# A gated recurrence with a slot mixture behind it: fillers placed elsewhere, two weight loads issued two units earlier, and the last weight loaded in two halves

## The chip, the cores and the metric

The kernel runs on one core of a Trainium2 chip. The metric is the device time of one execution in microseconds. The time before is the median of five runs.

## The reference

The inputs are `x` and `f_logit` of 4 x 5056 x 256 (batch, time, channel), a lower bound per channel, and the parameters of a mixture of experts with 32 slots: `phi` (256 x 32), eight first weights (256 x 1024) and eight second weights (1024 x 256). All are 32-bit floats.

```python
sig = 1.0 / (1.0 + np.exp(-f_logit))
f = lower_bound + (1.0 - lower_bound) * sig
for t in range(S):
    h = f[:, t] * h + (1.0 - f[:, t]) * x[:, t]
    y[:, t] = h
x = y.reshape(B * S, D)
logits = x @ phi
d = softmax over all tokens of logits          # per slot
slot_input = d.T @ x                           # 32 x 256
for e in range(8):                             # four slots each
    slot_out[e] = np.maximum(slot_input[e] @ w1[e], 0.0) @ w2[e]
c = softmax over the slots of logits           # per token
out = c @ slot_out
```

The softmax over tokens, and so the experts, need all tokens first. The kernel therefore has three stages: the recurrence with the slot sums, a short middle part with the experts, and the output, which writes 20224 rows of 256 values.

## The kernel before

**Units.** Time is cut into ten groups of 512 steps, and each group into four units, one for each batch element: 40 units (`n_unit`), numbered n. One pass of the main loop handles one n, with work of neighbouring units overlapped by hand; the order of instructions on every engine is the order in which the code issues them (`tc.manual_schedule()`).

In pass n the code calls, among others: `load(n + 6)` for two units at a time, which issues the reads of f_logit and x on SP's queue (lines 182 to 190, tiles `f_t` and `x_t`, three buffers each); `gate`, a sigmoid on ScalarE (line 200, tile `s_t`); `enter(n + 3)`, the product of gate and x on GpSimd, called POOL in the profile (line 211, tile `u_t`); `s_to_channels` and `u_to_channels`, transposes on TensorE (lines 213 to 226); `decay` on ScalarE (line 249); `scan`, the recurrence itself on VectorE (line 259, tile `h`); `to_tokens` and `keep_tokens`, transposes back and their copy (lines 272 and 289, tiles `hp` and `ht`).

**Exponential blocks.** The logits of two groups at a time go through one exponential (`exps`, line 312, tile `etall`). Then `weights_to_tokens` transposes them on TensorE (line 324), VectorE copies them (line 327), and `slots` adds the products with the tokens into `slot_ps` (line 353). In the loop this happens once in eight units: the transposes in a pass with n % 8 = 2, the slot sums of the block's two groups in the two passes behind it.

**Fillers.** `idle(k)` (lines 163 to 166) issues k matmuls that nobody reads. They write the second half of the bank whose first half is `slot_ps`. `spin(dst, k, w)` (lines 135 to 138) does the like with w columns, on the weight that is loaded first. The loop's fillers stand behind the transposes of a unit, at lines 473 to 476.

**Weights.** `load_w(i)` issues the read of one expert weight on POOL's queue, with a cast from 32 to 16 bits, 1 MB read and 512 KB written. Weights 0 to 7 are the first weights of the experts, 8 to 15 the second ones. `W_AT` says how many are issued in which pass, behind `enter` in POOL's order.

**The middle part.** Behind the loop, the last slot sums are scaled (line 541), the first weights are applied (line 559), and then the second ones: experts 0 to 3 together (line 595), and experts 4 to 7 one after the other (line 605, j = 0 to 3, eight matmuls each over the eight parts fc of the weight). Between j = 1 and j = 2 stand the last row sums (line 336) and `SPINS` fillers. Then VectorE scales the result (line 619, `slot_out`), and POOL makes the two-row form of it (line 621, `slot_bd`).

**The output.** `pieces`, `couple`, `rest` and `whole` multiply the exponentials with `slot_out` or `slot_bd` on TensorE (lines 639, 688 and 710), scale the rows on VectorE (lines 629 and 693) and ScalarE (lines 633 and 699), and issue the writes on SP's queue (lines 665, 676, 702 and 719). The PSUM bank in which the fillers write is given back to these tiles.

Of the kernel before, what the change touches and what calls it, by code (L numbers as in the profile page):

```python
# [18 lines left out]
def kernel(  # L19
# [10 lines left out]
    nc = tc.nc  # L30
    B, S, D = x.shape
    E = moe_w1.shape[0]
    F = moe_w1.shape[2]
    NS = moe_phi.shape[1]
    SPE = NS // E
    P = 128
    DC = D // P
    FC = F // P
# [3 lines left out]
    n_unit = n_grp * B  # L42
# [27 lines left out]
    ident = consts.tile([P, P], BF16, name="ident")  # L70
# [13 lines left out]
    def rep_constants(b):  # L84
        blk = ident_f[ds(b * NS, NS), ds(b * NS, NS)]
        nc.gpsimd.tensor_copy(rep[ds(b * NS, NS)], blk.unsqueeze(1).broadcast_to([NS, B, NS]))
# [33 lines left out]
    w2_r = moe_w2.rearrange("e (p fc) d -> e p fc d", p=P)  # L120
# [5 lines left out]
    w2_sb = [wts.tile([P, FC, D], BF16, name=f"w2_sb{e}") for e in range(E)]  # L126

    def load_w(i):
        if i < E:
            nc.gpsimd.dma_start(out=w1_sb[i], in_=w1_r[i])  # L130
        else:
            nc.gpsimd.dma_start(out=w2_sb[i - E], in_=w2_r[i - E])  # L132


    def spin(dst, k, w):
        for _ in range(k):
            nc.tensor.matmul(dst[:, ds(0, w)], w1_sb[0][:, 0, :P], w1_sb[0][:, 0, :w],
                             start=True, stop=True, skip_group_check=True)

    SPINS = 28  # L140
    W_AT = {17: 1, 25: 1, 30: 1, 31: 1, 32: 1, 33: 2, 34: 1, 36: 8}
    w_next = [0]
    ctx.enter_context(tc.manual_schedule())

# [3 lines left out]
    with tc.tile_pool(name="sp2", bufs=3) as sp2, \  # L148
# [9 lines left out]
        slot_bank = pslot.tile([P, 2, D], F32, name="slot_ps")  # L158
        slot_ps = slot_bank[:, 0]

        rep_bf = rep.rearrange("p b s -> p (b s)").bitcast(BF16)

        def idle(k, first=False):
            for i in range(k):
                nc.tensor.matmul(slot_bank[:, 1], ident, rep_bf,  # L165
                                 start=first and i == 0, stop=False, skip_group_check=True)
        xs, fs, sts, uts, pss, psus, hs, hps, hts, lgs, ets = ({} for _ in range(11))

        def tokens(src, n, k):
# [58 lines left out]
        def s_to_channels(n):  # L228
            if n % 2 == 0:
                pss[n // 2] = psp.tile([P, 2, P, R], F32, name="sp", tag="sp")  # L230
            to_channels(n, pss[n // 2][:, n % 2], sts[n // 2][:, n % 2],
                        sts[n // 2][:, 0, R3])
# [31 lines left out]
        SINGLE = 6  # L264
# [28 lines left out]
        def batch_of(g):  # L293
            return [g & ~1, g | 1] if g < n_grp - 2 else [g]
# [64 lines left out]
        def unit(f, m):  # L359
            if 0 <= m < n_unit:  # L360
                f(m)

        def group(f, m):
            if 0 <= m < n_unit and m % B == B - 1:
                f(m // B)

        def batch(f, m, i):
            m -= i
            if 0 <= m < n_unit and m % B == B - 1:
                gs = batch_of(m // B)  # L370
                if m // B == gs[-1] and i < len(gs):
                    f(gs[i])
# [52 lines left out]
        for n in range(n_unit):  # L425
            if n < SINGLE - 2:
                if n:
                    unit(to_tokens, n - 1)
                    unit(u_to_channels, n + 1)
                s_to_channels(n + 2)  # L430
                if n + 3 < SINGLE:
                    gate(n + 3, 1)
                decay(n + 2, 1)
                if n + 3 == SINGLE:
                    gate(n + 3)
                if n % 2 == 0:
                    unit(load, n + AHEAD)
                unit(enter, n + 3)
                rep_constants(n)
            else:  # L440
                end = n >= n_unit - 6
                if n % 2 == 0:
                    unit(load, n + AHEAD)
                    if n == SINGLE - 2:
                        to_tokens(n - 1)
                        keep_tokens(n - 1)
                    if not end:
                        unit(gate, n + 4)
                else:
                    unit(decay, n + 1)  # L450
                    if n == n_unit - 5:
                        gate(n + 3)
                        exps(odd - 1)
                if not end and n != n_unit - 7:
                    group(exps, n - 2)

                unit(enter, n + 3)
                for _ in range(W_AT.get(n, 0)):
                    load_w(w_next[0])
                    w_next[0] += 1  # L460

                if n == n_unit - 2:
                    unit(u_to_channels, n + 1)
                if n != SINGLE - 2:
                    unit(to_tokens, n - 1)
                if n == n_unit - 2:
                    keep_tokens(n - 1)
                if n % 2 == 0:
                    unit(s_to_channels, n + 2)
                    unit(s_to_channels, n + 3)  # L470
                if n != n_unit - 2:
                    unit(u_to_channels, n + 1)
                if n in (n_unit - 5, n_unit - 4):
                    idle(4)
                elif SINGLE - 2 < n < n_unit - 4 and n % (2 * B) in (1, 2, 5, 6, 7):
                    idle(5, n == SINGLE - 1)
                if n == n_unit - 2:
                    tail = psp.tile([P, 2, G], F32, name="tail", tag="sp")
                    rs_ps = tail[:, 0, ds(0, n_grp * R * B)].rearrange(
                        "p (q b) -> p q b", b=B)  # L480
                    late_ps, odd_ps = (
                        tail[:, 1].bitcast(BF16)[:, ds(i * R * P, R * P)].rearrange(
                            "p (r s) -> p r s", r=R) for i in range(2))
                    logits(odd)
                    exps(odd)
                    slots(odd - 1)
                    spin(tail[:, 1], 1, G)
                    odd_weights()
                elif not end:
                    group(logits, n - 1)  # L490
            if n == n_unit - 1:
                logits(last, [0, 1, 2])
                late_exps([0, 1, 2])
                row_sums(0)
                late_weights([0, 1, 2], nc.scalar.copy)

            unit(scan, n)
            if n not in (SINGLE - 2, n_unit - 2):
                unit(keep_tokens, n - 1)
            if n == n_unit - 3:  # L500
                weights_to_tokens(odd - 1)
                slots(odd - 2)
            elif not n >= n_unit - 6:
                group(weights_to_tokens, n - 3)
                batch(slots, n - 4, 0)
                batch(slots, n - 4, 1)
        hid, wide = (ld.tile([P, 2, R, D], F32, name=i, tag="x_t") for i in ("hid", "wide"))
        hid = hid.rearrange("p u r d -> p (u r d)").bitcast(BF16)[:, ds(0, FC * E // 2 * NS)]
        wide = wide.rearrange("p u r d -> p (u r d)").bitcast(BF16)[:, ds(0, FC * E // 2 * P)]
# [19 lines left out]
        for o in range(DC):  # L529
            nc.tensor.matmul(sin_ps[:, o], slot_v[:, o], rep[:, 0],  # L530
                             start=True, stop=True, skip_group_check=True)

    with tc.tile_pool(name="ew", bufs=1) as ew, \
# [18 lines left out]
        for q in range(E // Q):  # L552
            hi = ew.tile([P, F], BF16, name=f"hi{q}")
            for k in range(2):
                hi_ps = (psu.tile([P, H], F32, name="hi_ps", tag="up") if q == 0 else
                         pbig.tile([P, H], F32, name="hi_ps", tag=f"hi_ps{k}"))
                for o in range(DC):
                    for j in range(Q):
                        nc.tensor.matmul(hi_ps[ds(j * NS, NS)], sin[:, o],
                                         w1_sb[q * Q + j][:, o, ds(k * H, H)],  # L560
                                         start=(o == 0), stop=(o == DC - 1),
                                         skip_group_check=True)
# [30 lines left out]
        for e in range(Q):  # L593
            for fc in range(FC):
                nc.tensor.matmul(so4_ps[ds(fc % 4 * NS, NS), :], hid[:, fc, e],
                                 w2_sb[e][:, fc],
                                 start=(e == 0 and fc < 4),
                                 stop=(e == Q - 1 and fc >= FC - 4),
                                 skip_group_check=True)
# [3 lines left out]
        for j in range(Q):  # L603
            for fc in range(FC):
                nc.tensor.matmul(so_ps, wide[:, fc, j].rearrange("p b s -> p (b s)"),
                                 w2_sb[Q + j][:, fc],
                                 start=j == 0 and fc == 0, stop=j == Q - 1 and fc == FC - 1,
                                 skip_group_check=True)
            if j == 0:
                nc.tensor.matmul(so_ps, rep2, so4, start=False, stop=False,  # L610
                                 skip_group_check=True)
            if j == 1:
                for i in range(1, len(blocks)):
                    row_sums(i)
                q = n_grp * R - 1
                spin(tail[:, 1], SPINS, NS)
                nc.vector.reciprocal(rrow[:, wide_r:q], rs_ps[:, wide_r:q])
                nc.vector.reciprocal(rrow[:, q, ds(0, B // 2)], rs_ps[:, q, ds(0, B // 2)])
        nc.vector.tensor_scalar_mul(slot_out, so_ps, rcs)  # L619
        for u in range(2):  # L620
            nc.gpsimd.tensor_scalar_mul(slot_bd[:, u], slot_out, parity[:, ds(u, 1)])  # L621
# [139 lines left out]
```

## Time and profile before

| | us |
|---|---|
| median of five runs | 202.58 |
| lowest and highest | 201.61 and 203.11 |
| the profiled execution, its own time | 201.61 |
| its span | 199.8 |

| engine | busy us | share of the span |
|---|---|---|
| TensorE, matmuls (PE) | 141.7 | 71% |
| TensorE, weight loads (PEld) | 102.8 | 51% |
| VectorE (DVE) | 142.7 | 71% |
| ScalarE (ACT) | 137.9 | 69% |
| GpSimd (POOL) | 101.9 | 51% |

A profile gives for each engine its busy time, in 40 slices of the span a digit for the busy share in tenths, and for each group of instructions the mean duration and what ended the wait before it. The row PEclk is the clock that TensorE was granted, in tenths of full speed. The DMA row is the mean share of 16 DMA rings that were busy. A DMA with a cast counts in GB/s with the bytes that it writes. The chain that ended last follows the execution back from its end, from each step to what released it. Busy shares are means over three unlike stages, so the stages are read one by one.

### The profile page before, as it was taken

What the parts mean: (1) busy time and instruction counts of PE and PEld (TensorE: products, weight loads), DVE (VectorE), ACT (ScalarE), POOL (GpSimd) and SP (SyncE); (2) the same over time, 40 slices, a digit from 0 to 9 for tenths busy, and PEclk for the clock granted to TensorE, in tenths of its full rate; (3) what the DMA queues carried; (4) which work ended last, traced back from release to release, by engine and by line L of the source; (5) the groups of instructions that cost most, each with busy time, mean ns of one, the idle gap of its engine ahead of it and who ended that gap; (6) DMA issues with size and microseconds to landing.
All of it is one profiled execution on the core that took longest, in us unless ns stands there. A gap on an engine that the chain in (4) does not pass through costs nothing.

```text
span 199.8 us, 3263 instructions
## 1 busy us (share of the span) xinstructions
PE 141.7 (71%) x1201; PEld 102.8 (51%) x1201; DVE 142.7 (71%) x164; ACT 137.9 (69%) x194; POOL 101.9 (51%) x76
## 2 busy tenths in 40 slices
PE   0587564986988959777888778999679999970000
PEld 0365443965776847665776666667653533420000
DVE  1669878699999998999999999342167887850000
ACT  2688675899998997999996694621057889990000
POOL 2589595874999296983998779900030000000000
PEclk9999999699999988999999999999985555555555
DMA  5999999999999999999999999999529999999994
GB/s 177 417 420 420 420 421 415 420 420 417 416 419 419 335 394 421 419 405 307 419 415 275 252 217 197 216 212 215 111 98 394 416 449 430 420 423 436 453 420 213
DMA packets 17615, 70.76 MB, mean 354 GB/s; under 512 B 2096, under 2 KB 3120, under 8 KB 16704
## 3 DMA queue, kind: packets, MB, share of 16 engines
q1 hardware_dynamic: 15120, 62.13, 76.1%
q0 software_dynamic: 2336, 8.42, 21.1%
q8 instruction: 9, 0.15, 0.3%
q14 instruction: 6, 0.05, 0.1%
q10 hardware_dynamic: 144, 0.00, 0.0%
HBM read 58.23 MB, written 20.71 MB: 395 GB/s over the span
## 4 chain that ended last, share of the span: by engine, by line
PE 28%; DVE 22%; DMA 18%; issue 11%; POOL 6%; ACT 4%; SPq 0%; DVEq 0%; ACTq 0%; POOLq 0%
DVE h L259 18%; PE op L688 12%; DMA w_sb<-in_moe_w_dram 10%; DMA f_t<-in_f_logit_dram 8%; POOL u_t L211 4%; PE hp L272 3%; PE sp L226 3%; PE op L639 3%; DVE ht L289 3%; PE up L226 2%; POOL w_sb L132 2%; ACT oc L699 1%; PE slot_ps L165 1%; ACT a L249 1%; DVE et L327 1%
## 5 line engine op out<-in xcount | busy, mean ns | idle before, releaser
L211 POOL TENSOR_TENSOR u_t<-s_t,x_t 128x1024 bf16<-128x1024 bf16 (+1 forms) x39 | 82.2, 2124 | 24.8 <-ACT s_t L200 19.6
L259 DVE TENSOR_TENSOR_SCAN h<-a,h,up 128x512 bf16<-128x512 f32 (+1 forms) x72 | 86.0, 1249 | 4.0 <-PE up L226 2.4
L249 ACT ACTIVATE a<-sp,nomlb 128x1024 f32<-128x1024 bf16 (+2 forms) x46 | 43.2, 990 | 4.0 <-PE sp L226 3.0
L200 ACT ACTIVATE s_t<-f_t 128x2048 bf16<-128x2048 f32 (+2 forms) x23 | 38.4, 1671 | 9.6 <-DMA f_t<-in_f_logit_dram 7.2
L272 PE MATMUL hp<-ident_f,h 128*128 128x128 f32 (+1 forms) x160 | 29.6, 309 | 19.9 <-DVE ht L289 16.1
L272 PEld LDWEIGHTS hp<-ident_f,h 128*128 128x128 f32 (+1 forms) x160 | 22.8, 208 | 28.6 <-DVE ht L289 19.9
L226 PE MATMUL sp<-ident_f,s_t 128*128 128x128 f32 x144 | 21.8, 296 | 11.4 <-ACT s_t L200 7.9
L688 PE MATMUL op<-slot_bd,etall 64*128 64x512 bf16 x62 | 24.9, 622 | 0.2 <-ACT oc L699 0.2
L226 PEld LDWEIGHTS sp<-ident_f,s_t 128*128 128x128 f32 x144 | 17.9, 153 | 13.2 <-issue 6.0
L226 PE MATMUL up<-ident_f,u_t 128*128 128x128 f32 x144 | 24.2, 294 | 0.6 <-POOL u_t L211 0.6
L699 ACT ACTIVATE oc<-op,rrow 128x256 f32<-128x256 f32 x60 | 22.7, 488 | 2.2 <-PE op L688 1.7
L693 DVE TENSOR_TENSOR oc<-op,rrow 128x1024 f32<-128x1024 f32 x16 | 19.3, 1222 | 5.4 <-PE op L688 5.4
L226 PEld LDWEIGHTS up<-ident_f,u_t 128*128 128x128 f32 x144 | 18.3, 152 | 1.8 <-POOL u_t L211 1.2
L688 PEld LDWEIGHTS <-etall 64*128 64x128 bf16 x62 | 9.0, 155 | 14.8 <-issue 12.7
L289 DVE COPY ht<-hp 128x512 f32<-128x512 f32 (+1 forms) x22 | 14.7, 667 | 2.4 <-PE hp L272 2.4
L165 PE MATMUL slot_ps<-rep,ident 128*128 128x256 bf16 x108 | 16.0, 279 | 0.0
L289 ACT COPY ht<-hp 128x512 f32<-128x512 f32 (+1 forms) x18 | 10.5, 582 | 6.3 <-PE hp L272 6.2
L633 ACT ACTIVATE ob<-op,rrow 128x256 f32<-128x256 f32 x16 | 6.3, 480 | 11.3 <-PE op L639 11.2
L165 PEld LDWEIGHTS <-ident 128*128 128x128 bf16 x108 | 10.8, 100 | 1.2
L259 DVE TENSOR_TENSOR_SCAN h<-a,up 128x512 bf16<-128x512 f32 x8 | 9.3, 1208 | 2.4 <-ACT a L249 1.7
L621 POOL TENSOR_SCALAR slot_bd<-slot_out,parity 128x256 bf16<-128x256 bf16 x2 | 1.8, 918 | 16.1 <-DVE slot_out L619 16.1
L303 PE MATMUL lg<-h,phi 128*32 128x512 bf16 (+1 forms) x80 | 7.3, 413 | 0.0
(98 smaller groups left out, 126.0 us busy)
## 6 DMA issues: line engine op xcount, KB each, us to landing
f_t<-in_f_logit_dram SPq DMA_DIRECT2D x36, 512.0 KB, 9.9
x_t<-in_x_dram SPq DMA_DIRECT2D x36, 512.0 KB, 9.9
out_dram<-oc SPq DMA_DIRECT2D x6, 2048.0 KB, 12.7
w_sb<-in_moe_w_dram POOLq DMA_DIRECT2D x16, 512.0 KB, 10.2
out_dram<-oc SPq DMA_DIRECT2D x4, 896.0 KB, 5.2
out_dram<-ob SPq DMA_DIRECT2D x1, 2048.0 KB, 8.4
f_t<-in_f_logit_dram SPq DMA_DIRECT2D x4, 384.0 KB, 8.3
x_t<-in_x_dram SPq DMA_DIRECT2D x4, 384.0 KB, 8.2
```

The lines of the kernel that those rows point to most:

```text
L165: nc.tensor.matmul(slot_bank[:, 1], ident, rep_bf, start=first and i == 0, stop=False, skip_group_check=True)
L200: nc.scalar.activation(s_t, f_t, ACT.Sigmoid, scale=-1.0)
L211: nc.gpsimd.tensor_tensor(uts[n][:, :r], s_t[:, :r], x_t[:, :r], ALU.mult)
L226: nc.tensor.transpose(ps[:, :, r], t[:, r], ident_f)
L249: nc.scalar.activation(decays[n // 2, o][:, ds(n % 2, k), :T], sp[:, ds(n % 2, k), :T, o], ACT.Identity, scale=nomlb[:, ds(o, 1)], bias=1.0)
L259: nc.vector.tensor_tensor_scan(h[:, :T, o], decays[n // 2, o][:, n % 2, :T], up[:, :T, o], hs[n - B][:, ds(used(n // B - 1) - 1, 1), o] if ...
L272: nc.tensor.transpose(hp[:n_p, r], hw[:, :n_p, r], ident_f)
L289: copy(hts[g][:n_p, b].rearrange("p r d -> p (r d)").bitcast(F32), hps.pop(n)[:n_p].rearrange("p r c -> p (r c)"))
L303: nc.tensor.matmul(lg[ds(b * NS, NS), :], phi[:, o], hs[g * B + b][:, :T, o], start=o == 0, stop=o == DC - 1, skip_group_check=True)
L688: nc.tensor.matmul(op[:, i_r].rearrange("p u d -> p (u d)"), ew[:, :, r + i_r], slot_bd[ds(j * 2 * NS, 2 * NS)].rearrange("s u d -> s (u d)"),
L693: nc.vector.tensor_tensor(ob[:, :, ds(r, k)].rearrange("p u r d -> p r u d"), op[:, ds(0, k)], scale[:, ds(r, k)].unsqueeze(3).broadcast_t ...
L699: nc.scalar.activation(ob[:, u, r + i_r], op[:, i_r, u], ACT.Copy, scale=scale[:, r + i_r, ds(u, 1)])
```

## The change

Four things are edited.

1. `W_AT`: three weights instead of one are issued in pass 34, and six instead of eight in pass 36.
2. `load_w`: the last weight (15) is read with two DMAs, each with four of its eight parts, so that each row is 4 KB instead of 8 KB.
3. `idle` in the loop: the five fillers in passes with n % 8 = 2 go; pass 4 gets six, with 128 columns of the identity; passes 11, 19 and 27 get eight behind their slot sums.
4. `spin`: between j = 1 and j = 2 there are 14 fillers of 128 columns instead of 28 of 32, and four of 256 columns follow behind j = 3, ahead of the scaling on VectorE in the code.

```diff
         else:
-            nc.gpsimd.dma_start(out=w2_sb[i - E], in_=w2_r[i - E])
+            k = FC // 2 if i == 2 * E - 1 else FC
+            for f in range(0, FC, k):
+                nc.gpsimd.dma_start(out=w2_sb[i - E][:, ds(f, k)], in_=w2_r[i - E][:, ds(f, k)])
...
-    SPINS = 28
-    W_AT = {17: 1, 25: 1, 30: 1, 31: 1, 32: 1, 33: 2, 34: 1, 36: 8}
+    SPINS = 14
+    W_AT = {17: 1, 25: 1, 30: 1, 31: 1, 32: 1, 33: 2, 34: 3, 36: 6}
...
         def idle(k, first=False):
+            rhs = ident if first else rep_bf
             for i in range(k):
-                nc.tensor.matmul(slot_bank[:, 1], ident, rep_bf,
-                                 start=first and i == 0, stop=False, skip_group_check=True)
+                nc.tensor.matmul(slot_bank[:, 1, ds(0, rhs.shape[1])], ident, rhs,
+                                 start=first and i < 2, stop=False, skip_group_check=True)
...
-                elif SINGLE - 2 < n < n_unit - 4 and n % (2 * B) in (1, 2, 5, 6, 7):
-                    idle(5, n == SINGLE - 1)
+                elif n == SINGLE - 2:
+                    idle(6, True)
+                elif n < n_unit - 4 and n % (2 * B) in (1, 5, 6, 7):
+                    idle(5)
...
                 batch(slots, n - 4, 1)
+                if n > 2 * B and n % (2 * B) == 3:
+                    idle(8)
...
-                spin(tail[:, 1], SPINS, NS)
+                spin(tail[:, 1], SPINS, P)
...
+        spin(tail[:, 1], 4, D)
         nc.vector.tensor_scalar_mul(slot_out, so_ps, rcs)
```

## The prediction

> **What bounds the kernel now.** I read the page's slices first, then the chain that ended last, then the stages from 112 to 150 us in windows of 1 us and as a timeline, and at last the DMA packet records of the trace.
>
> ```profile
> span 199.8 us, 3263 instructions
> ...
> PEclk9999999699999988999999999999985555555555
> DMA  5999999999999999999999999999529999999994
> ...
> HBM read 58.23 MB, written 20.71 MB: 395 GB/s over the span
> ```
>
> A slice is 5 us. The DMA row is full from 5 to 140 us, falls to 5 and 2 around the turn from reading to writing (140 to 150), and is full again to the end. 58.23 MB at the 420 GB/s that most input slices show are 138.6 us; 20.71 MB are 49.3 us. The whole time is reading, a turn, and writing. What is saved in the loop beside reading is worth nothing; the end of reading and the turn can be shortened.
>
> ```profile
> 120.44 3.71 POOL w_sb L132 x7
> 124.16 0.00 issue
> 124.16 20.38 DMA w_sb<-in_moe_w_dram
> 144.54 0.04 issue
> 144.59 1.05 PE so_ps L605 x8
> ```
>
> The chain passes from the last weight's issue through 20.38 us of transfer to the eight matmuls that use it. The windows (DMA share and GB/s are the last two columns; casting loads are counted by what they write, half of what they read) show where the weight stream has holes:
>
> ```profile
> 121.00:122.00 1.00, 0.57 (x17) 0.36 (x17) 1.00 (x2) 0.00 (x0) 1.00 (x2) 1.00 1.15 209
> 122.00:123.00 1.00, 1.00 (x12) 0.92 (x8) 1.00 (x2) 0.00 (x0) 1.00 (x3) 1.00 0.91 156
> 123.00:124.00 1.00, 1.00 (x26) 0.55 (x25) 1.00 (x2) 0.85 (x2) 1.00 (x3) 1.00 1.01 201
> ...
> 142.00:143.00 1.00, 0.85 (x8) 0.77 (x8) 0.76 (x2) 0.00 (x0) 0.00 (x0) 1.00 0.50 98
> 143.00:144.00 1.00, 0.18 (x2) 0.01 (x1) 0.00 (x0) 0.00 (x0) 0.00 (x0) 1.00 0.09 16
> 144.00:145.00 1.00, 0.41 (x4) 0.37 (x4) 0.00 (x0) 0.00 (x0) 0.00 (x0) 1.00 0.00 0
> ```
>
> At 122 the rate falls from about 209 to 156; after 143 only a straggler is left. The timeline around both:
>
> ```profile
> 112.86 0.58 POOL L130 DMA_DIRECT2D w_sb<-in_moe_w_dram  x1
> ...
> 116.20 4.25 POOL L211 TENSOR_TENSOR u_t<-s_t,x_t 128x1024 bf16<-128x1024 bf16 x2 [2.77 <-issue]
> ...
> 120.40 4.30 POOL L132 DMA_DIRECT2D w_sb<-in_moe_w_dram  x8
> ...
> 142.15 1.03 PE L605 MATMUL so_ps<-w_sb,wide 128*128 128x256 bf16 x8 [0.17 <-DMA w_sb<-in_moe_w_dram]
> ...
> 144.59 1.03 PE L605 MATMUL so_ps<-w_sb,wide 128*128 128x256 bf16 x8 [1.41 <-DMA w_sb<-in_moe_w_dram]
> ...
> 145.66 0.48 DVE L619 TENSOR_SCALAR slot_out<-so_ps,rcs 128x256 bf16<-128x256 f32 x1 [2.89 <-PE so_ps L605]
> 146.19 0.37 PE L639 MATMUL op<-slot_out,etall 32*128 32x256 bf16 x2 [0.57 <-DVE slot_out L619]
> ```
>
> The reader is to see POOL idle for 2.77 us before 116.20, the eight issues only after both u_t products, and TensorE idle for 1.41 us before its last eight matmuls.
>
> **Part 1, two weights at unit 34.** I number weights 0 to 15. Weight 7 is issued at 112.86; 8 and 9 now follow it, two issues of 0.58 us in POOL's 2.77 us of idleness. Queued behind them is the product of unit 38, which starts at 116.20, when its x_t has landed (last packet 116.17); so the move costs POOL nothing. Does it delay that x_t? In 105 to 112 us the weight queue and the input queue put through about 35 and 34 packets a us: they alternate. Weights 4 to 7 were still unfinished when the x_t ended, so the weight queue had work all along, and two more weights behind it change no turn. SP issues no input after 101.93 and is not passed.
>
> What it brings: by its completion packets weight 7 ends on the earliest of 16 DMA rings at 121.60, weight 8 at 124.66; in the stream behind, one weight takes 2.46 us a ring. So these rings stood for 0.6 us, waiting for descriptors that POOL began at 120.40. The latest rings (123.08 to 123.54, then 125.54 to 126.00) never stood. The last weight waits for the slowest ring alone: 144.23, the next 143.50, the always-fed ones 143.20 at most. Each 16 KB instruction packet sets one ring back by about 1.1 us (116.43, 130.69, 139.40). Weight 8 also shows one ring more among the late ones than weight 7 had, with a packet of 1.26 us at 122.04 where 0.32 is usual. If this is the ring that is last at 144.23, the gain is down to the always-fed 143.20, or 1.0 us; if the last one was always fed, nothing. Instruction packets seem to go round the rings, each time to one that was not yet late, and this speaks for the first. I take 0.7 us, and keep 0 and 1.0.
>
> **Part 2, the last weight in halves.** POOL issues once more (0.56 us), but two went to unit 34: its memsets come 0.55 us earlier, beside other work. The transfer: 128 rows of 8 KB read become 256 of 4 KB. Nearest row: packets of 2 KB in the output took 84 ns against 159 for 4 KB, so two cost 9 ns or 6% more: 0.06 x 2.46 = 0.14 us, and 0.02 for the second completion packet. Bounds: 0 and +0.3. In return four matmuls come before the second landing. Eight take 1.03 us with 0.27 for one alone, so (1.03 - 0.27) / 7 = 0.109 each; four are 0.43. Net -0.43 + 0.16 = -0.27; bounds -0.43 and +0.3 (nothing if the reader waits for both halves).
>
> A rule speaks against this part. The Trainium skill, "DMA: Bandwidth & Descriptors", section "Anatomy of one DMA", fits a DMA by some 2.0 us plus its bytes at 436 GB/s, and its rules for authors want 1 MiB or more a transfer. Paid once more, 2.0 us would make this part +1.6 instead of -0.27. But here each weight follows the last at 2.46 us on its ring, where 1 MB by the fit is 4.4: in a queue the fixed part is already hidden, and I keep the trace's price.
>
> **Part 3, fillers and spins.** The loop's fillers were 108 (20 units of 5, two of 4). Four units lose 5 (10, 18, 26, 34); unit 4 gets 6 of half width, units 11, 19 and 27 get 8 each behind the slot sums: 108 - 20 + 6 + 24 = 118. Five of 256 columns take 0.71 us, so eight take about 1.04. After the slot sums at 48.06 TensorE waits until 50.16 for a VectorE copy; the eight fit. The five removed stood ahead of the transposed exponentials, so VectorE's wait of 0.20 us there goes. All of it lies beside a full DMA, with inputs issued about 9.9 us before they land: 0, and if that cover were gone, at most 3 x 1.04. The clock's dips at 36 and 74 us may go too, also for nothing.
>
> The spins between weights 13 and 14 change from 28 of 32 columns (0.85 us) to 14 of 128 (14 x 0.054 = 0.76), beside a wait for weight 14: 0. The four new ones of 256 columns (0.43 us) fall into the 0.57 us in which TensorE waits for slot_out: 0, at worst +0.2. TensorE's total stays at 1201 (+10 - 14 + 4).
>
> Might these spins hold the clock in the output? The row shows 0.5 from 148.6 to the end, though TensorE is shown fully busy from 150 to 178. The skill, "TensorE: Matmul & The Clock Gate", Part 1, has the clock come back after about 3.4 us of sustained work. By it, the before would be fast again by 153 and the spins could win a few us of ramp; by the row, output matmuls on 32 and 64 rows did not bring it back. Even when held, the output is DMA-bound: DMA stands open only in 148.5 to 149.5 (0.25, 0.79) and 153.5 to 154.5 (0.81, 0.57), together 0.8 us of which I would give half to the clock. I take 0 and keep -0.5.
>
> **Sum.** -0.7 - 0.27 + 0 = -0.97 us, rounded to -1.0. The profiled execution took 201.61 us (span 199.8 and 1.8 around it); it is the lowest of the five, 0.97 under the median of 202.58. Against it I get 200.6; as a median, 201.6.
>
> **Rivals.** B: the slowest ring was always fed, part 1 brings nothing: -0.3, 202.3. For it: the spread of landings by the instruction packets alone; against: the extra late ring. C: everything, the clock too: -1.0 - 0.43 + 0.16 - 0.5 = -1.8, 200.8. For it: more columns where the clock fell; against: the four spins add 0.43 us of work to a stretch of about 3.4 us, the length of a dip in the loop. D, slower: the two early weights get in front of the last x_t. Place: units 38 and 39, whose products, scans and last sums follow from 116.20. Price: up to two weights, 2 x 2.46 = 4.9 us. Without waits for weights the last eight matmuls could start at about 142.5 (141.97 - 0.46 + 0.99), 2.1 before they do; only a delay over 3.1 makes the end more than 1.0 later, and the full price gives +2.8, 205.4. For it: inputs and weights do share every ring; against: the weight queue had a backlog of 1.6 weights when x_t ended. That the splitting does nothing is inside B.
>
> **How the numbers follow.** A (the sum) 0.55, B 0.17, C 0.12, D 0.16. About 0.5%, or 1.0 us, is what a measurement of this kernel can tell from no change. A spreads from -0.5 to -1.5 around the border; I give 0.6 of it to faster. Faster 0.55 x 0.6 + 0.12 = 0.45; same 0.55 x 0.4 + 0.17 = 0.39; slower 0.16. The range reaches from a little below C, for the spread of the runs, to just past the border of D: 200.4 to 203.4; D's upper end is left out.
>
> **What would show it.** Right: no fall of the rate at 122; the last landing near 143.5 instead of 144.54; four matmuls of line 605 behind it instead of eight; first output some 1.0 us earlier; the writing stage still about 50 us. Wrong: the x_t of unit 38 landing after 117 (D); the last landing still near 144.5 (B); the output stage at full clock with a steeper start (C); or a hole in the DMA row before 140.

## The result and the profile after

The changed kernel takes 201.04 us as the median of 43 runs (199.87 to 202.20), the kernel before 202.97 us over the 80 runs that stood beside them (200.40 to 207.48). The ratio is 0.9936, with a 95% interval of 0.9920 to 0.9953: 0.64% less, or 1.3 us (1.0 to 1.6). The ratio compares the fast runs alone; runs of the kernel before that took over 1.5% longer than its fastest are left out, so the two medians lie further apart (1.9 us) than the ratio says. The forecast was 1.0 us less.

The two profiled executions show no gain. Before's took 201.61 us, near the low end of its runs; after's took 201.99, near the high end of its own. They are read for what waits on what; how much it is worth comes from the timed runs.

The page of the changed kernel, in the lines that were shown of before:

```profile
span 200.2 us, 3264 instructions
...
PEclk9999889999999999999999957999995555555555
DMA  6999999999999999999999999999529999999994
...
HBM read 58.23 MB, written 20.71 MB: 394 GB/s over the span
```

Reading, a turn and writing, as before. The clock's second dip is not near 74 us any more, but at 115 to 122.

The windows at the places where before had its hole (the last two columns are the DMA share and GB/s):

```profile
121.00:122.00 1.00, 1.00 (x6) 1.00 (x5) 1.00 (x2) 0.91 (x1) 0.01 (x1) 0.50 1.07 221
122.00:123.00 1.00, 0.82 (x10) 0.60 (x9) 1.00 (x3) 0.00 (x0) 0.32 (x1) 0.90 1.08 217
123.00:124.00 1.00, 0.40 (x16) 0.34 (x16) 1.00 (x2) 0.00 (x0) 1.00 (x1) 1.00 1.02 205
...
142.00:143.00 1.00, 1.00 (x19) 1.00 (x18) 0.00 (x0) 0.00 (x0) 0.00 (x0) 1.00 0.67 121
143.00:144.00 1.00, 1.00 (x22) 1.00 (x21) 0.00 (x0) 0.00 (x0) 0.00 (x0) 1.00 0.21 37
```

At 122 to 123 the rate is 217 where it was 156. But the timeline shows something that was not forecast:

```profile
110.12 0.58 POOL L130 DMA_DIRECT2D w_sb<-in_moe_w_dram  x1
...
110.70 1.07 POOL L134 DMA_DIRECT2D w_sb<-in_moe_w_dram  x2
...
115.08 1.91 ACT L203 ACTIVATE s_t<-f_t 128x2048 bf16<-128x2048 f32 x1 [3.55 <-DMA f_t<-in_f_logit_dram]
...
118.87 2.14 POOL L214 TENSOR_TENSOR u_t<-s_t,x_t 128x1024 bf16<-128x1024 bf16 x1 [7.10 <-DMA x_t<-in_x_dram]
...
122.68 2.14 POOL L214 TENSOR_TENSOR u_t<-s_t,x_t 128x1024 bf16<-128x1024 bf16 x1 [1.67 <-DMA x_t<-in_x_dram]
...
144.17 1.91 PE L612 MATMUL so_ps<-w_sb,wide 128*128 128x256 bf16 x16
...
146.12 0.48 DVE L627 TENSOR_SCALAR slot_out<-so_ps,rcs 128x256 bf16<-128x256 f32 x1 [0.99 <-PE so_ps L612]
```

The loop is ahead (weight 7 is issued at 110.12 instead of 112.86), yet POOL waits 7.10 and 1.67 us for the last two x_t, the last of which ends at 122.20 instead of 116.17. From there the work runs through to line 612 (605 before), whose last sixteen matmuls come in one go and wait for no weight. The chain that ended last says the same: its longest piece is now an input.

```profile
99.39 23.13 DMA x_t<-in_x_dram
...
122.68 2.15 POOL u_t L214
...
144.34 1.76 PE so_ps L612 x16
```

### The profile page after: what moved, and what is told of

Its sections match the earlier page's. It is cut to its first block, busy times and chain, and to the rows that moved or that the text cites. A ratio compares the mean times of both kernels' runs of the same rounds, so it can differ in the third digit from the quotient of the medians.

```text
span 200.2 us, 3264 instructions
## 1 busy us (share of the span) xinstructions
PE 144.6 (72%) x1201; PEld 105.3 (53%) x1201; DVE 142.4 (71%) x164; ACT 137.8 (69%) x194; POOL 102.4 (51%) x77
## 4 chain that ended last, share of the span: by engine, by line
DMA 42%; PE 25%; ACT 11%; issue 5%; DVE 4%; POOL 1%; SPq 0%; ACTq 0%; DVEq 0%; POOLq 0%
DMA x_t<-in_x_dram 27%; DMA f_t<-in_f_logit_dram 16%; PE op L696 12%; ACT a L252 4%; ACT s_t L203 3%; DVE h L262 3%; PE op L647 2%; PE so_ps L612 2%; ACT oc L707 1%; POOL u_t L214 1%; PE tail L139 1%; PE hp L275 1%; PE tail L339 1%; PE hi_ps L566 1%; ACT L203 1%
## 5 line engine op out<-in xcount | busy, mean ns | idle before, releaser
L229 PE MATMUL sp<-ident_f,s_t 128*128 128x128 f32 x144 | 23.2, 309 | 13.4 <-ACT s_t L203 11.1
L229 PEld LDWEIGHTS sp<-ident_f,s_t 128*128 128x128 f32 x144 | 18.7, 159 | 15.5 <-ACT s_t L203 5.9
L229 PE MATMUL up<-ident_f,u_t 128*128 128x128 f32 x144 | 24.7, 298 | 1.4 <-POOL u_t L214 1.4
L229 PEld LDWEIGHTS up<-ident_f,u_t 128*128 128x128 f32 x144 | 18.9, 156 | 2.8 <-POOL u_t L214 2.1
L168 PEld LDWEIGHTS <-ident 128*128 128x128 bf16 x118 | 11.5, 101 | 1.9 <-issue 0.6
```

Of the source, the lines that this page charges most:

```text
L168: nc.tensor.matmul(slot_bank[:, 1, ds(0, rhs.shape[1])], ident, rhs, start=first and i < 2, stop=False, skip_group_check=True)
L229: nc.tensor.transpose(ps[:, :, r], t[:, r], ident_f)
```

## The experiments

Each experiment changes a part of the kernel and is timed against the kernel before; a ratio below 1 is faster, and the interval behind it is the 95% one. Times inside an execution are from its profile. Two theories stood at first. **W** is the prediction's: the end is the last weight's landing, and the weights' schedule and the halves bring it forward. **F** came from the profile after: the loop's fillers carry the gain, since the loop runs ahead and a dip of the clock is gone. Each part alone separates them.

### The weights alone

```diff
-    W_AT = {17: 1, 25: 1, 30: 1, 31: 1, 32: 1, 33: 2, 34: 1, 36: 8}
+    W_AT = {17: 1, 25: 1, 30: 1, 31: 1, 32: 1, 33: 2, 34: 3, 36: 6}
```

> The kernel before with the schedule of weights alone changed (three at pass 34, six at pass 36). Theory W (the prediction's: the last weight lands earlier): the last landing moves from 144.5 to about 143.5 us, ratio to before 0.9965 (bounds 0.995 and 1.0). Theory F (the loop's fillers carry the gain, since the last stretch is bound by when the last x_t lands and by how many clock dips the loop has): ratio 0.999 to 1.002, with a spread of runs as wide as before.

Ratio 0.9958 (0.9934 to 0.9983), and the runs lie within 200.32 to 203.15 instead of 200.24 to 205.28. In the windows the hole is gone:

```profile
121.00:122.00 1.00, 0.66 (x17) 0.44 (x18) 1.00 (x2) 0.00 (x0) 1.00 (x3) 1.00 1.08 217
122.00:123.00 1.00, 1.00 (x12) 0.88 (x16) 1.00 (x2) 0.00 (x0) 1.00 (x2) 1.00 1.04 209
123.00:124.00 1.00, 1.00 (x26) 0.60 (x25) 1.00 (x2) 0.93 (x2) 0.03 (x1) 1.00 1.06 213
```

The last weight's last packet ends at 143.57 instead of 144.23. This is what theory W expected, and outside what F did.

### The halves alone

```diff
-            nc.gpsimd.dma_start(out=w2_sb[i - E], in_=w2_r[i - E])
+            k = FC // 2 if i == 2 * E - 1 else FC
+            for f in range(0, FC, k):
+                nc.gpsimd.dma_start(out=w2_sb[i - E][:, ds(f, k)], in_=w2_r[i - E][:, ds(f, k)])
```

> The kernel before with the last weight alone read in two halves. Theory W: four matmuls fewer behind the last landing, 0.27 us less, ratio 0.9987. Theory F: nothing in most runs, ratio 0.999 to 1.001. If halves cost a fixed price of their own (2 us), ratio 1.008.

Ratio 0.9973 (0.9942 to 1.0004): compatible with -0.27 us, not resolved from nothing, and a fixed price of 2 us is excluded. The matmuls are split as forecast, four behind each landing, and the second four take 0.60 us where eight took 1.03:

```profile
143.64 0.60 PE L607 MATMUL so_ps<-w_sb,wide 128*128 128x256 bf16 x4 [0.25 <-DMA w_sb<-in_moe_w_dram]
...
144.84 0.60 PE L607 MATMUL so_ps<-w_sb,wide 128*128 128x256 bf16 x4 [0.60 <-DMA w_sb<-in_moe_w_dram]
```

### The loop's fillers alone

`idle` itself is edited as in the whole change; the places where it is called:

```diff
-                elif SINGLE - 2 < n < n_unit - 4 and n % (2 * B) in (1, 2, 5, 6, 7):
-                    idle(5, n == SINGLE - 1)
+                elif n == SINGLE - 2:
+                    idle(6, True)
+                elif n < n_unit - 4 and n % (2 * B) in (1, 5, 6, 7):
+                    idle(5)
...
+                if n > 2 * B and n % (2 * B) == 3:
+                    idle(8)
```

> The kernel before with the loop's fillers alone changed (none at n % 8 = 2, six at pass 4, eight behind the slot sums). Theory W: no effect, ratio 1.0. Theory F: no dip of the clock near 74 us in the profile, pass 25 (second weight issued) near 84 us instead of 86.5, a narrower spread of runs, ratio 0.993 to 0.996; the earlier weights then share the DMA rings with the last inputs, so the x_t of unit 39 lands after 118 us instead of 116.2.

Ratio 1.0115 (1.0083 to 1.0146), slower by 2.3 us. Theory F is wrong on the time, though right on what it said of the loop: no dip near 74, the second weight issued at 84.61, and the last x_t at 121.95. What costs is behind it. The timeline of POOL, then the windows:

```profile
110.42 0.57 POOL L130 DMA_DIRECT2D w_sb<-in_moe_w_dram  x1
...
122.44 2.15 POOL L212 TENSOR_TENSOR u_t<-s_t,x_t 128x1024 bf16<-128x1024 bf16 x1 [1.68 <-DMA x_t<-in_x_dram]
...
124.53 4.29 POOL L132 DMA_DIRECT2D w_sb<-in_moe_w_dram  x8
```

```profile
122.00:123.00 1.00, 0.99 (x9) 0.78 (x7) 0.70 (x2) 0.00 (x0) 0.56 (x1) 0.60 0.48 94
123.00:124.00 1.00, 0.23 (x8) 0.23 (x12) 0.97 (x2) 0.00 (x0) 1.00 (x1) 1.00 0.19 37
124.00:125.00 1.00, 0.75 (x19) 0.47 (x9) 1.00 (x2) 0.00 (x0) 1.00 (x2) 1.00 0.00 0
125.00:126.00 1.00, 1.00 (x15) 0.79 (x17) 1.00 (x2) 0.18 (x1) 1.00 (x3) 1.00 0.19 33
126.00:127.00 1.00, 1.00 (x25) 0.44 (x17) 1.00 (x2) 0.98 (x3) 1.00 (x3) 1.00 0.83 127
```

Weights 0 to 7 are done by 124.09, the other eight stand in POOL's order behind the product that waits for the late x_t, and the rings lose some 3.3 us (what is missing to 1 in the DMA share from 122 to 127). In before the same hole was 0.6 us, on the earliest rings only.

### The spins alone, and two tests of what they cost

```diff
-    SPINS = 28
+    SPINS = 14
...
-                spin(tail[:, 1], SPINS, NS)
+                spin(tail[:, 1], SPINS, P)
...
+        spin(tail[:, 1], 4, D)
```

> The kernel before with the fillers of the middle part alone changed (14 of 128 columns instead of 28 of 32, four of 256 columns behind the last weight's matmuls). Both theories: ratio 0.999 to 1.001. If the spins hold the clock in the output: clock row above 0.5 past 152 us and ratio 0.997. If they delay the first output matmuls: ratio 1.001.

Ratio 1.0052 (1.0023 to 1.0081), which neither theory had. In this profile slot_out starts at 144.97, earlier than in before, and the first output is issued at 146.59. Then SP's third issue takes 2.24 us, where the third of before took 0.42. SP's timeline around that one issue, of this kernel and of before:

```profile
147.73 2.24 SPq L666 DMA_DIRECT2D out_dram<-ob  x1
```

```profile
148.44 0.42 SPq L665 DMA_DIRECT2D out_dram<-ob  x1
```

The packet records have the ninth 16 KB packet of the instruction queue at 147.65, of 1.95 us; in before it came at 146.07, ahead of the outputs. TensorE had then started 2215 matmuls and weight loads here and 2211 in before. This kernel has ten spins fewer, so about the same count is reached later in the program. Theory **I**: the packet stalls the issue. Theory **S**: the spins themselves do.

```diff
-    SPINS = 28
+    SPINS = 24
...
-                spin(tail[:, 1], SPINS, NS)
+                spin(tail[:, 1], SPINS, P)
...
+        spin(tail[:, 1], 4, D)
```

> The spins alone, as in the run before, with ten more of them (24 of 128 columns instead of 14), so that TensorE's program is as long as before. Theory I (a 16 KB packet of TensorE's instructions that comes as the first outputs are issued stalls SP's third issue; ten instructions fewer moved it from 146 to 147.7 us): the packet is back at 145 to 146, no output issue takes over 1 us, ratio 0.996 to 1.000. Theory S (the four spins themselves hold up the output): ratio stays at 1.004 to 1.006.

With `SPINS = 24` the ratio is 0.9998 (0.9972 to 1.0025); its interval just touches that of the spins alone. The packet starts at 146.79, later than the expectation had it, but the whole profiled execution is late: the first output is issued at 149.66, and no output issue stalls. The other way round, ten of the old spins are left out and nothing else is changed:

```diff
-    SPINS = 28
+    SPINS = 18
```

> The kernel before with ten of the 28 spins left out and nothing else. Theory I (the length of TensorE's program sets when its last 16 KB instruction packet comes): the packet starts after 147 us, where the first outputs are issued, one output issue of SP takes over 1.5 us, ratio 1.003 to 1.006. Rival (the spins themselves were what cost in the run of the spins alone): ratio 0.998 to 1.000.

The packet starts at 150.21 and the third output issue takes 1.83 us:

```profile
150.24 1.83 SPq L665 DMA_DIRECT2D out_dram<-ob  x1
```

Both runs speak for theory I. The ratio, 1.0103 (1.0054 to 1.0152, from six runs), is more than it asked for. In this profile the clock dips five times in the loop, pass 36 issues its weights at 123.21 instead of 120.40, and the first ring is done with weight 8 at 127.56 instead of 124.66: the hole of the fillers' run once more. How much of the 1% is the packet and how much the hole stays open.

### What the fillers do beside the early weights

First the fillers and the schedule of weights together, without halves and spins; to the diff of the fillers comes

```diff
-    W_AT = {17: 1, 25: 1, 30: 1, 31: 1, 32: 1, 33: 2, 34: 1, 36: 8}
+    W_AT = {17: 1, 25: 1, 30: 1, 31: 1, 32: 1, 33: 2, 34: 3, 36: 6}
```

> The kernel before with the loop's fillers and the schedule of weights, but the last weight whole and the spins as before. Theory H (the fillers alone lost because all rings stood still from 122 to 128 us, waiting for the eight weights behind a late x_t; the two weights at pass 34 fill just this hole): ratio 0.994 to 0.999 against 1.0115 for the fillers alone, weight 8 done on all rings by 126.5 instead of 129.3. Rival (the fillers cost TensorE or VectorE time on the path): ratio above 1.005.

Ratio 0.9944 (0.9920 to 0.9968). The x_t is as late as with the fillers alone (121.89), but weight 8 is done on the last ring at 126.48 and not at 129.34. Two weights issued at pass 34 turn +1.15% into -0.56%, as theory H of the expectation had it.

Then the whole change with the old fillers in the loop and ten spins more, which keeps TensorE's total; against the changed kernel (`idle` is as in before):

```diff
-    SPINS = 14
+    SPINS = 24
...
-                elif n == SINGLE - 2:
-                    idle(6, True)
-                elif n < n_unit - 4 and n % (2 * B) in (1, 5, 6, 7):
-                    idle(5)
+                elif SINGLE - 2 < n < n_unit - 4 and n % (2 * B) in (1, 2, 5, 6, 7):
+                    idle(5, n == SINGLE - 1)
...
-                if n > 2 * B and n % (2 * B) == 3:
-                    idle(8)
```

> The whole change without the loop's fillers (they stay as before), with 24 spins of 128 columns so that TensorE's program is as long as before. Theory N (the loop's fillers bring nothing, weights and halves bring all): ratio 0.990 to 0.994, the same as the whole change or better, x_t of unit 39 landing near 117. Theory C (fillers and early weights only work together): ratio 0.996 to 0.998, worse than the whole change (0.9936).

Ratio 0.9924 (0.9899 to 0.9950), against 0.9936 for the whole change: theory N, and not C. Without the new fillers the x_t lands at 115.47, slot_out starts at 144.70, and the span is 198.7 us.

At last only the two diffs of the weights and of the halves, with the spins as before:

```diff
+            k = FC // 2 if i == 2 * E - 1 else FC
...
+    W_AT = {17: 1, 25: 1, 30: 1, 31: 1, 32: 1, 33: 2, 34: 3, 36: 6}
```

> Weights and halves only: the loop's fillers and the spins as before. Theory N (these two parts carry the whole gain): ratio 0.991 to 0.995, not worse than the whole change (0.9936). Theory C (fillers and spins add to it): ratio 0.996 to 0.998.

Ratio 0.9940 (0.9913 to 0.9966), again as theory N had it. Two of the four parts give the whole gain, as far as the intervals tell. The weights alone, at 0.9958, are not told apart from the two, and the profile does not show the halves at work: TensorE, which waits for nothing from 137 us on, reaches the last sixteen matmuls at 143.81, when the last packet (143.58) is in.

```profile
143.81 1.91 PE L607 MATMUL so_ps<-w_sb,wide 128*128 128x256 bf16 x16
```

The same block of sixteen without a wait stands in the profiles of the fillers and weights, of all but the loop's fillers, of the whole change, and of the schedule with four weights at pass 34 below. There TensorE is no longer ahead of the last landing, and the halves have little left to save.

### Other schedules

The first is set into the changed kernel:

```diff
-    W_AT = {17: 1, 25: 1, 30: 1, 31: 1, 32: 1, 33: 2, 34: 3, 36: 6}
+    W_AT = {17: 1, 25: 1, 34: 6, 36: 8}
```

> The whole change with other passes for the weights: none at 30 to 33, six at 34, eight at 36, so that no weight shares the rings with the last inputs before about 110 us. Theory X (in the changed kernel the last stretch is bound by the x_t of unit 39, which lands at 122.2 because weights take two thirds of each ring): x_t lands by 116, the last weight's matmuls wait for its landing again, slot_out starts near 144.7 instead of 146.1, ratio 0.987 to 0.990. Rival (the bytes bound the end whatever their order): ratio 0.992 to 0.995. If the rings run dry between inputs and weights: a hole near 112 us and a ratio over 1.0.

Ratio 1.0126 (1.0077 to 1.0176). Half of theory X holds: with no weight in the rings between 91.8 and 109 us the last x_t lands at 108.76, 13 us earlier than in the changed kernel. But the expectation for dry rings came true as well:

```profile
106.00:107.00 1.00, 1.00 (x12) 0.89 (x10) 1.00 (x2) 0.59 (x1) 1.00 (x1) 1.00 0.98 401
107.00:108.00 1.00, 0.32 (x4) 0.10 (x2) 1.00 (x3) 0.00 (x0) 1.00 (x2) 1.00 0.39 160
108.00:109.00 1.00, 1.00 (x10) 1.00 (x11) 1.00 (x2) 0.36 (x1) 1.00 (x1) 1.00 0.11 45
109.00:110.00 1.00, 0.91 (x9) 0.67 (x7) 0.99 (x2) 0.66 (x2) 1.00 (x3) 1.00 0.00 0
```

The rings stand still for about 3 us, and the last packet of the last weight ends 3.1 us after the changed kernel's (147.04 against 143.90).

And in the kernel with weights and halves only:

```diff
-    W_AT = {17: 1, 25: 1, 30: 1, 31: 1, 32: 1, 33: 2, 34: 3, 36: 6}
+    W_AT = {17: 1, 25: 1, 30: 1, 31: 1, 32: 1, 33: 2, 34: 4, 36: 5}
```

> Weights and halves only, but four weights at pass 34 and five at pass 36. If the hole behind weight 7 still opens in executions where pass 36 comes late: a narrower spread than with three, ratio 0.990 to 0.993. If three already cover it: the same ratio as with three, 0.991 to 0.995. If four delay the last x_t: above 0.996.

With four at pass 34 and five at 36 the ratio is 0.9936 (0.9910 to 0.9961): three already cover the hole.

Side by side, from the packet records and timelines of the profiled executions:

| kernel | ratio | last x_t packet | weight 8 done, first to last ring | last weight's last packet | slot_out starts |
|---|---|---|---|---|---|
| before | 1 | 116.17 | 124.66 to 126.00 | 144.23 | 145.66 |
| weights alone | 0.9958 | 117.47 | 123.99 to 126.37 | 143.57 | 145.53 |
| fillers alone | 1.0115 | 121.95 | 128.49 to 129.34 | 147.66 | 149.09 |
| fillers and weights | 0.9944 | 121.89 | 124.14 to 126.48 | 143.69 | 145.74 |
| weights and halves | 0.9940 | 115.88 | 123.96 to 126.32 | 143.58 | 145.75 |
| all but the loop's fillers | 0.9924 | 115.47 | 124.20 to 125.91 | 143.31 | 144.70 |
| the whole change | 0.9936 | 122.20 | 124.08 to 126.49 | 143.90 | 146.12 |

The five without a hole behind weight 7 end the last weight within 0.6 us of each other, however late x_t was. None of them is told apart from the whole change by its interval.

## Why the prediction was right, point by point

**The bound.** Right: reading, turn, writing. The output's DMA packets add up to 49.3 us over 16 rings in before and in after.

**Part 1, -0.7 us.** Alone it measured -0.42%, or 0.9 us (0.3 to 1.3). The hole at 122 was the reason, as forecast, and the last packet moved by 0.7 us in the profile. The packet records of before also settle what the prediction left between 0 and 1.0 us: the ring that ends last, at 144.23, is the extra late one. The records do not number the rings, but its lag can be followed: it stays 1.24 us behind the first ring from weight 8 to 13, and the instruction packet at 139.41 sets it back to 2.37. So by the prediction's own argument 1.0 us was the right end, and that packet did not go to a ring that was not yet late. What the prediction did not see is that its profile showed the hole near its smallest. The hole is the time in which the first ring stands between weights 7 and 8. In the six executions traced with the old schedule, in the order of pass 36 (120.28 to 124.53 us), it was 0.5, 0.6, 1.1, 1.3, 2.1 and 4.4 us; the last two are the run with five dips of the clock and the one with the late x_t. In the six with three or four weights at pass 34 it was 0.0. So the early weights are an insurance, worth most in an execution where pass 36 comes late. That the hole is what makes the longer runs of before long is not shown, since none of these was traced.

**Part 2, -0.27 us.** Alone -0.5 us, with an interval from -1.2 to +0.1. The saving of 0.43 us in matmuls is in the trace (1.03 to 0.60). The price is not settled as finely: the halves' packets took 173 ns, 7% more than half of 324, as estimated; but the slowest ring needs, for the last two weights, 4.96 us in the run of weights and halves, 5.12 in the whole change and 5.42 in the run of the halves alone, where two whole weights are 4.92. That is +0.05 to +0.5, against 0.16 and an upper bound of 0.3, and instruction packets have a part in it that was not separated. The price of 2 us for one more DMA, which the prediction weighed by the Trainium skill ("DMA: Bandwidth & Descriptors", "Anatomy of one DMA"), does not appear in this full queue, where the interval ends at +0.1. In the changed kernel's own profile the halves save nothing, because the matmuls are late for another reason, and in the run of weights and halves they did not wait either. So this term is seen in the run of the halves alone, and not in the sum that it was added to.

**Part 3, fillers 0.** This term was right in the sum and wrong in its reason. The prediction said that they lie beside a full DMA, so that nothing follows. They made the loop faster: the second weight is issued at 84.61 alone and at 84.03 in the whole change, instead of 86.50. But the bytes that DMA has read by a given time are the same (44.5 MB by 110 us in before and with the fillers alone), so weights issued earlier take their turns from inputs still to come (41.0 MB of these are inputs in before, 40.3 with the fillers), and the last x_t lands 6 us later. Alone that costs 2.3 us. This is inside the 3.1 us that was kept as the worst case, but not by its reason: it is not what the fillers cost, but what a faster loop triggers. Only because weights 8 and 9 are issued in the same change does it come to about nothing.

**Part 3, spins 0.** Right for the whole change, but by luck. The clause that TensorE's total stays at 1201 names the condition, and the prediction drew nothing from it. Alone, with ten matmuls fewer, the spins cost 0.5%, by the place of an instruction packet, as far as the two tests show.

**The clock.** C did not come: the row falls to 0.5 at 149.5 us, 1.1 us later than before, and stays there to the end, some 50 us.

**Rival D.** Its sign that the prediction is wrong, an x_t after 117, was seen at 122.20. The cause is not the one named, two weights at pass 34 in front of x_t. With the old fillers x_t lands at 116.17 to 117.51 in five executions without the early weights and at 115.47 to 117.47 in four with them; with the new fillers and the same loads at passes 30 to 33 it lands at 121.89 to 122.20, with them or without. The old executions also show that 117 was no sharp border. (The queue held more than the 1.6 weights that the prediction counted against D: by the bytes, 2.6 were still to be read when before's x_t ended.) Nor did the full price come: x_t is 6.0 us later, but the last product starts 4.4 us later (122.68 against 118.30, since before's waited behind that of unit 38), and VectorE, which in before still had older scans to do, ends its last scan 2.2 us later (128.26 against 126.08). That is about the room of 2.1 us that D counted, and slot_out starts 0.46 us later than in before.

**The signs.** Of those that were to show it right, the fall of the rate at 122 is gone, the last packet is at 143.90, and the writing still takes 50 us (148.6 to 198.5). The other two did not come: sixteen matmuls stand where four were to stand behind the last landing, and the first output is issued at 147.74 instead of 147.28, not 1.0 us earlier.

**The sum.** The four parts alone multiply to 0.9958 x 0.9973 x 1.0115 x 1.0052 = 1.0098; together they are 0.9936. The mechanism of part 1 is confirmed and carries the gain; that the total came out near 1.0 us is in part luck, because two of its zeros are zeros only together with the rest, and because the hole is larger in most of the other traced executions than in the one that was read.

## What to carry to other kernels

Where transfers of two kinds share full rings, as here, an engine that gets ahead does not move more bytes; it changes whose bytes come last, so ask which issue waits behind the one that is now late. Put enough of the second kind into the queue ahead of that wait that the rings do not run dry in an execution that runs late, and look at several executions before a hole's size is taken from one. A part that costs nothing in the sum should be tried alone: here one such part cost 1.15% by itself.

## What the runs showed of the hardware

A 16 KB packet of the instruction queue is not free. In the weight stream it sets one ring back by about 1.1 us (from 1.24 to 2.37 behind the first in before). When it came among the first output issues, SP's issue took 2.24 or 1.83 us instead of 0.42. Leaving ten filler matmuls out, which shortens TensorE's work, moved that packet into the output's start. That these packets carry TensorE's program is inferred: in all thirteen kernels the ninth came when TensorE had started 2185 to 2221 matmuls and weight loads, at times from 144.69 to 150.21 us.

POOL's last issue, the second half of weight 15, also waited for weight 8, eight loads earlier, by 1.92 us in the run of weights and halves. It had no effect on the end, since the rings were busy with the weights between until about 140 us:

```profile
126.92 0.53 POOL L134 DMA_DIRECT2D w_sb<-in_moe_w_dram  x1 [1.92 <-DMA w_sb<-in_moe_w_dram]
```
